# Two load orders and a new set of plan priorities in a convolution-and-attention kernel

## The chip, the core and the metric

The kernel runs on one core of one Trainium2 chip. A core has TensorE (PE; its weight loads are shown apart as PEld), VectorE (DVE), ScalarE (ACT), GpSimd (POOL) and SyncE (SP), each of which takes its own instructions in order. SP, and here and there POOL and ACT, issue DMAs. The metric is the device time of one execution in microseconds (us); less is better. Times of the program are the median of several executions, and one execution is recorded by the hardware profiler.

## What is computed

Two branches work on the same input x (`A_q`, 2048 rows of 640) and are mixed by a gate:

```
g = sigmoid((x * gate_w).sum(-1))
kv = (4-tap causal convolution of A_k along the rows) * A_v
y = irfft(rfft(kv padded to 4096) * rfft(ssm_k padded to 4096))[:2048] + kv * ssm_D
a = x * y
q, k, v = x @ wqkv                     # 32 heads of 20
b = softmax(q . k over 8 keys, 2 rows apart, backwards) @ v, then @ wo
out = g * a + (1 - g) * b
```

Branch a is a long convolution of each of 640 channels; branch b is attention in a narrow dilated window.

## The kernel before

**Stages.** In the order in which they mostly run:

- x is transposed (`trx`), projected to v (`psv`, in two halves of the columns, evicted to `VW`) and to q and k (`pj`, evicted to `Gs` and `sH`). `fragger` (L616) moves pieces of q and k by POOL DMAs into sets of four heads (`qb`, `kb`), eight sets in all, three buffers.
- For each set `score_gen` computes scores (`sc`), ScalarE exponentiates them (L676, `ET`), `pv_gen` multiplies by v (`O`), and VectorE normalises into `oS` (L714, L716).
- VectorE meanwhile makes kv by `conv` in four row blocks, from block 3 down to block 0 (taps and additions of 1.49 us each). Each finished block is stored to DRAM (`st..`), from where kv is loaded again in another layout (`kv<-kv_scr`).
- The filter `ssm_k` is loaded in two halves (`load_h`, each eight DMAs of 160 KB in runs of 128 bytes) over the space of k in `Hb`; POOL adds ssm_D to it (`h_diag`, L802, once for each half).
- `transform` does a two-stage Fourier transform, first of the filter ("h", into `Hs`), then of kv ("u", into `X`): first-stage units (L738) and second-stage units (L760). The second stage multiplies by the matrix G, loaded into `Gs` once the pieces of q and k there are moved. Groups 0 to 2 of five make pass 0, groups 3 and 4 pass 1.
- `swaps` (L826) copies each transformed filter group with its two partition halves exchanged (the turned spectrum). The copy of group 4 is made in two halves, since its place in `X` is group 0's turned copy; its first half is issued after product block 1 of pass 0, its second half after block 3 (events m01, m03).
- `mults` (L848) forms the products in place: L858 (spectrum by spectrum into Hs) and L862 (by the turned copy into X), four blocks for each pass. L858 overwrites what the swap reads.
- `inverse1` (L865) needs the products of its pass: 20 units of 16 matmuls, twelve for pass 0, eight for pass 1. `inverse2` (L930) needs all of inverse1, the table T (`load_t`, after the last product m13) and q, which `load_q` (L903) brings and `qscale` (L923) scales by the gate.
- `otrans` (L885) transposes oS into `Hb` (`tr`), `outproj` (L978) multiplies by wo (`op`), ScalarE scales to `room`, POOL DMAs bring that to `bl`, `adds` adds it to q times y, and the sums are stored.

**What sets the order.** Nothing of it is written out by hand. Each stage is a generator that asks for an engine with a cost and a list of events it depends on (`Req`); `Plan.run` (L208) always grants the request with the smallest start time plus 120 ns times the priority of its generator (`PR`, L146, less is sooner), and only then is the instruction emitted. So each engine's program order comes out of the plan's own clock. A `"S"` request is a DMA on SP's queue, `"G"` a step on POOL. Evictions ask for "AD": ScalarE or VectorE, whichever the plan's clock has ready first; the `..lean` entries shift that choice. An event that a request waits for is a time in the plan. On the chip the waits are those that the data need (a tile written, read, or reused). The plan also hands out the four pairs of PSUM banks.

Of the kernel before, what the change touches and what calls it, by code (L numbers as in the profile page):

```python
# [142 lines left out]
LAT = {("P", "A"): 230.0, ("P", "D"): 230.0, ("A", "P"): 120.0, ("D", "P"): 120.0, ("A", "D"): 100.0, ("D", "A"): 100.0}  # L143


PR = {'warm': -10.0, 'loads': 0.0, 'o_slot': -41.5, 'fragger': -30.7, 'score_gen': -0.4, 'pv_gen': -0.8, 'masks': 1.1, 'wcopy': 3.5, 'halo_gen': -13.7, 'conv': 17.2, 'transposes': 1.3, 'vproj': 2.4, 'gate': 2.4, 'qkproj': 3.1, 'h_diag': 16.3, 'h_stream': 1.9, 'open_p3': 26.5, 'swaps': -47.2, 'u_stream': 7.3, 'mults': -6.7, 'inverse1': 11.0, 'otrans': 10.8, 'outproj': 6.2, 'load_t': 18.2, 'load_q': 8.6, 'qscale': 0.8, 'adds': -3.0, 'inverse2': 25.0, 'vproj1': 4.5, 'vevict': -4.9, 'qevict': -6.0, 'opearly': 14.6, 'oplate': 22.1, 'vlean': 5.0, 'qlean': -169.0, 'slean': 204.0, 'ilean': 93.0, 'olean': 20.0, 'uh': 17.9}  # L146
HEAD = dict(A=130.0, D=60.0)


# [100 lines left out]
def kernel(  # L250
# [91 lines left out]
    def ev(name):  # L342
        if name not in E:
            E[name] = Ev()
        return E[name]
# [10 lines left out]
    def loads():  # L356
        def load(name, dst, src, nb, run, deps=()):
            g = yield Req("S", 300.0 + nb / run * 0.5, deps, move=us(nb, run))
            nc.sync.dma_start(dst, src)
            mark(name, g)  # L360

        def load_x(c, k0=0, k1=4):
            yield from load(f"x{c}{k0}", xS[:, 4 * c + k0:4 * c + k1, :], xq4[:, c // 2, 4 * (c % 2) + k0:4 * (c % 2) + k1, :],
                            163840 * (k1 - k0), 1280)

        def nat(src, a):
            return raw(src, 4 * a * D, [[16 * D, 128], [1, 4 * D]])

        yield from load("ident", ident[:], ca["ident"].ap(), 32768, 256)
        yield from load_x(0, 0, 2)  # L370
        yield from load_x(0, 2, 4)
        yield from load("Wv0", Wv[:, :, 0:320], W3[:, :, 2, 0:320], 409600, 640)
        yield from load_x(1)
        yield from load_x(2)
        yield from load_x(3)
        def load_w(w, part, c0, c1):
            yield from load(f"W{w}{part}", Wqk[:, :, w, c0:c1], W3[:, :, w, c0:c1], 1280 * (c1 - c0), 2 * (c1 - c0))

        def load_k(a):
            yield from load(f"k{a}", Hb[:, 4 * a * D:4 * (a + 1) * D], nat(k2, a), 655360, 5120)  # L380

        def load_v(a):
            yield from load(f"v{a}", kvs[:, 4 * a * D:4 * (a + 1) * D], nat(v2, a), 655360, 5120, [ev("vgo")])

        for part, c0, c1 in (("a", 0, 128), ("b", 128, D)):
            for w in range(2):
                yield from load_w(w, part, c0, c1)
            if part == "a":
                yield from load("wr", pa[:].rearrange("p t c -> p (t c)"), raw(A_shift_k, 0, [[0, 128], [1, 4 * D]]), 655360, 5120)
        yield from load_k(3)  # L390
        yield from load_k(2)
        yield from load_v(3)
        yield from load_k(1)
        yield from load_v(2)
        yield from load_k(0)
        yield from load_v(1)
        yield from load_v(0)
        yield from load("Wv1", Wv[:, :, 320:640], W3[:, :, 2, 320:640], 409600, 640)

        def load_h(half):  # L400
            deps = [ev(f"st{a}{c}") for a in ((2, 3) if half == 0 else (0, 1)) for c in range(2)]
            for q in range(4):
                for c in range(2):
                    yield from load(f"h{half}{q}{c}", st["hv"](half)[32 * q:32 * q + 32, :, c, :],
                                    raw(A_ssm_k, (160 * q + 80 * c + 40 * half) * S, [[64, 32], [S, 40], [1, 64]]), 163840, 128, deps)

        def store_kv(a):
            src = Hb[:, 4 * a * D:4 * (a + 1) * D].rearrange("p (q c x) -> p q c x", q=4, c=2)
            for c in range(2):
                yield from load(f"st{a}{c}", raw(kv_scr[:], (4 * c * S + 4 * a) * 80, [[16 * 80, 128], [S * 80, 4], [1, 320]]),  # L410
                                src[:, :, c, :], 327680, 640, [ev(f"conv{a}")])

        yield from store_kv(3)
        yield from store_kv(2)
        yield from load_h(0)
        yield from store_kv(1)
        yield from store_kv(0)
        for jb in range(4):
            for d, h in zip(pieces(Gs[:, 2048 * jb:2048 * (jb + 1)]), pieces(cf["G"].ap()[:, 2048 * jb:2048 * (jb + 1)])):
                yield from load(f"G{jb}", d, h, 262144, 1024, [ev("stg21"), ev("stg30"), ev("stg31")])  # L420
            ev(f"G{jb}").t += 2000.0
        yield from load_h(1)
        stored = [ev(f"st{a}{c}") for a in range(4) for c in range(2)]
        for c in range(2):
            for m in range(4):
                yield from load(f"kv{c}", kvs[:, 5120 * c + 1280 * m:5120 * c + 1280 * (m + 1)],
                                raw(kv_scr[:], c * 4 * S * 80 + 1280 * m, [[5120, 128], [1, 1280]]), 327680, 2560, stored)
        wo = p0.tile([128, NDT, D], BF, name="wo", tag="wo")
        st["wo"] = wo
        yield from load("wo", wo[:], B_wo.rearrange("(t p) n -> p t n", p=128), 819200, 1280, [ev("vproj1")])  # L430
# [185 lines left out]
    def fragger():  # L616
        todo = {}
        for t in range(NT):
            for w in range(2):
                for h in range(4 * t, 4 * t + 4):  # L620
                    for f in range(DH * h // 128, (DH * h + DH - 1) // 128 + 1):
                        todo.setdefault(t, []).append((f, w, h))
        rest = {}
        for v in todo.values():
            for f, w, h in v:
                rest[(f, w)] = rest.get((f, w), 0) + 1
        for t in range(NT):
            for f, w, h in sorted(todo[t]):
                yield Req("G", 1.0, [ev(f"pj{f}{w}")])
                stg, evs, free = stgs[(f, w)]  # L630
                f0 = 128 * f
                wd = QW if w == 0 else KW
                fa, fb = max(DH * h, f0), min(DH * h + DH, f0 + 128)
                r0 = 32 * (h % 4) + fa - DH * h
                dst = (qsets if w == 0 else ksets)[t % 3]
                deps = list(evs) + ([ev(f"sc{t - 3}")] if t >= 3 else [])
                g = yield Req("G", 510.0, deps, move=us((fb - fa) * wd * 2, 4200) * 1.9)
                nc.gpsimd.dma_start(dst[r0:r0 + fb - fa, 0:wd], stg[fa - f0:fb - f0, 0:wd])  # L638
                if (t, f, w, h) == (0, 0, 1, 3):
                    nc.gpsimd.memset(kvs[0:1, 12 * D:12 * D + 1], 0.0)  # L640
                    mark("vgo", g)
                rest[(f, w)] -= 1
                if not rest[(f, w)]:
                    free.t, free.eng = g.done.t, "X"
                    mark(f"stg{f}{w}", g)
            mark(f"set{t}", g)
        mark("frag", g)


# [176 lines left out]
    def swaps():  # L826

        for g in range(NG):
# [10 lines left out]
            for hf in range(2):  # L839
                yield Req("S", 0.0, deps + [ev(f"m0{2 * hf + 1}")])  # L840
                for p in (0, 64):
                    r = yield Req("S", 700.0, move=us(262144, 512) * 1.9)
                    d, h = (x.rearrange("p (m n) -> p m n", n=512)[:, :, 256 * hf:256 * hf + 256] for x in (turned(g)[p:p + 64], st["HA"][64 - p:128 - p, g, :]))
                    nc.sync.dma_start(d, h)
                for k in range(2):
                    mark(f"hw{g}{2 * hf + k}", r)

    def mults():  # L848
        for ps_, (g0, n, m) in enumerate(PASS):
# [51 lines left out]
        st["bl"] = bl  # L901

    def load_q():  # L903
        yield Req("G", 1.0, [ev("us1")])
        qg = p0.tile([128, 16, D], BF, name="qg", tag="kv")
        st["qg"] = qg
        for a in range(2):
            for g in range(4):
                r = yield Req("S", 900.0, [ev("us1")], move=us(327680, 1280) * 1.4)
                for t in range(2):  # L910
                    nc.sync.dma_start(st["qg"][32 * g:32 * g + 32, 8 * a + t:8 * a + 8:2, :],
                                      raw(x2, (16 * g + 8 * a + t) * D, [[64 * D, 32], [2 * D, 4], [1, D]]))
            mark(f"qg{a}", r)
            ev(f"qg{a}").t += 3000.0
# [167 lines left out]
```

## Time and profile before

| | us |
|---|---|
| median of 5 runs | 241.79 |
| lowest and highest run | 239.98, 243.14 |
| the profiled execution | 241.57 |
| its span, first to last instruction | 239.8 |

Busy time in four stretches of the profiled execution (us of 20):

| from to | PE | DVE | ACT | PE clock | DMA share |
|---|---|---|---|---|---|
| 20 to 40 | 19.5 | 12.2 | 15.4 | 1.00 | 0.77 |
| 80 to 100 | 19.8 | 16.2 | 18.5 | 1.00 | 0.31 |
| 100 to 120 | 15.5 | 15.3 | 18.0 | 0.57 | 0.98 |
| 160 to 180 | 18.0 | 18.7 | 20.0 | 1.00 | 0.82 |
| 200 to 220 | 20.0 | 9.0 | 12.8 | 0.96 | 0.30 |

The clock is the share of full speed that TensorE was granted. An engine that is busy all the time in a stretch sets its length, or one that it waits for does; the busy share alone doesn't say which, and a matmul's end is modelled.

The exponentials (L676) end at 127.4. The first second-stage unit of the filter starts at 130.8, the first of kv at 155.8. The products of pass 0 end at 179.7, those of pass 1 at 198.8; inverse1 ends at 207.8, the last out projection at 225.9.

### The profile page before, as it was taken

The page shows a single profiled execution, that of the slowest core. Times are in us where ns is not written, and L with a number is a line of the kernel's source. Part 1 is how long each engine was busy: PE and PEld are TensorE (multiplying, and loading weights), DVE is VectorE, ACT ScalarE, POOL GpSimd, SP SyncE. Part 2 cuts the span into 40 slices and gives each one's busy share as a digit, 9 for nine tenths or more (in the row PEclk, how much of TensorE's full clock was granted, in tenths as well). Part 3 has the DMA queues.
Part 4 walks back from the last instruction along what each step waited for, and adds up shares of the span by engine and source line. Part 5 has one row for each costly group of instructions (what it writes and reads, how often), then busy time and mean ns, then how long its engine had stood idle before and what let it go on. Part 6 is the DMA issues. An engine that isn't in the chain of part 4 may idle for free. (4 is left out here: it accounts for less than half of the span.)

```text
span 239.8 us, 8121 instructions
## 1 busy us (share of the span) xinstructions
PE 209.4 (87%) x3526; PEld 157.3 (66%) x3526; DVE 172.5 (72%) x214; ACT 183.6 (77%) x225; POOL 67.8 (28%) x137
## 2 busy tenths in 40 slices
PE   7999999999999999887875989989899969999800
PEld 3865645555555566575655778878689959989700
DVE  0667457998797797877774999999998095069760
ACT  4439588779899898889994998999999965943520
POOL 8803711396706053140000000000303020047520
PEclk9999999999999999955555899999999997999955
DMA  6997499677779622499899708996599916015872
GB/s 187 355 329 286 105 303 320 210 186 204 204 141 188 180 53 63 123 188 207 149 152 284 281 3 184 204 202 119 117 218 200 182 30 207 13 57 160 233 217 56
DMA packets 52579, 42.57 MB, mean 178 GB/s; under 512 B 27216, under 2 KB 47824, under 8 KB 52544
## 3 DMA queue, kind: packets, MB, share of 16 engines
q1 hardware_dynamic: 47664, 32.70, 56.6%
q0 software_dynamic: 4688, 9.03, 14.5%
q8 instruction: 27, 0.44, 0.9%
q10 hardware_dynamic: 192, 0.33, 0.5%
q14 instruction: 8, 0.07, 0.1%
HBM read 23.51 MB, written 5.25 MB: 120 GB/s over the span
## 5 line engine op out<-in xcount | busy, mean ns | idle before, releaser
L676 ACT ACTIVATE ET<-sc 128x726 bf16<-128x726 f32 (+1 forms) x80 | 64.9, 862 | 5.8 <-PE sc L668 5.4
L602 PE MATMUL pj<-xT,Wqk 128*128 128x363 bf16 (+3 forms) x250 | 48.4, 343 | 0.0
L1004 POOL DMA_DIRECT2D bl<-room x32 | 16.7, 528 | 81.7 <-ACT room L995 81.7
L602 PEld LDWEIGHTS <-Wqk 128*128 128x128 bf16 x250 | 22.9, 97 | 18.4
L279 DVE CAST Hs<-s 128x1024 bf16<-128x1024 f32 (+1 forms) x26 | 28.6, 1144 | 4.4 <-PE s L738 4.3
L277 ACT CAST X<-s 128x1024 bf16<-128x1024 f32 (+1 forms) x32 | 28.0, 997 | 0.2 <-PE s L738 0.2
L540 PE MATMUL psv<-Wv,xT 128*128 128x320 bf16 x170 | 24.9, 299 | 0.0
L988 PE MATMUL op<-wo,Hb 128*128 128x320 bf16 x160 | 23.9, 301 | 0.6 <-ACT X L277 0.5
L875 PE MATMUL i<-M,Hs 128*128 128x128 bf16 x160 | 21.9, 235 | 2.5 <-DVE Hs L858 2.3
L277 ACT CAST X<-i 128x1024 bf16<-128x1024 f32 x20 | 19.8, 1080 | 4.8 <-PE i L875 4.8
L875 PEld LDWEIGHTS <-Hs 128*128 128x128 bf16 x160 | 20.9, 151 | 2.6 <-DVE Hs L858 2.5
L668 PE MATMUL sc<-qb,kb 31*128 31x121 bf16 x544 | 18.7, 242 | 4.4 <-ACT ET L676 1.2
L875 PE MATMUL i<-M,X 128*128 128x128 bf16 x160 | 21.8, 235 | 0.5 <-DVE X L862 0.5
L988 PEld LDWEIGHTS <-Hb 128*128 128x128 bf16 x160 | 21.3, 145 | 1.3 <-issue 0.4
L760 PEld LDWEIGHTS <-Gs 64*128 64x128 bf16 x512 | 18.4, 95 | 5.3 <-issue 4.6
L875 PEld LDWEIGHTS <-X 128*128 128x128 bf16 x160 | 20.8, 151 | 0.8 <-DVE X L862 0.7
L995 ACT ACTIVATE room<-op,omg 128x640 bf16<-128x640 f32 x16 | 13.2, 825 | 10.3 <-PE op L988 8.6
L638 POOL DMA_DIRECT2D qb<-Gs x21 | 11.5, 551 | 31.7 <-ACT Gs L277 20.3
L668 PEld LDWEIGHTS <-kb 31*128 31x128 bf16 x544 | 10.3, 102 | 15.3 <-issue 12.5
L540 PEld LDWEIGHTS <-xT 128*128 128x128 bf16 x170 | 16.0, 98 | 6.6 <-issue 0.2
L277 ACT CAST Hs<-s 128x1024 bf16<-128x1024 f32 (+1 forms) x18 | 15.4, 912 | 3.7 <-PE s L738 2.3
L702 PEld LDWEIGHTS <-ET 128*128 128x128 bf16 x544 | 16.0, 100 | 3.4 <-issue 1.9
(77 smaller groups left out, 351.4 us busy)
## 6 DMA issues: line engine op xcount, KB each, us to landing
X<-Hs SPq DMA_DIRECT2D x16, 256.0 KB, 6.5
Hb<-in_A_k_dram SPq DMA_DIRECT2D x4, 640.0 KB, 10.4
kv<-in_A_v_dram SPq DMA_DIRECT2D x4, 640.0 KB, 12.3
kv_scr<-Hb SPq DMA_DIRECT2D x8, 320.0 KB, 4.4
Hb<-in_A_ssm_k_dram SPq DMA_DIRECT2D x16, 160.0 KB, 4.5
kv<-kv_scr SPq DMA_DIRECT2D x8, 320.0 KB, 5.0
bl<-room POOLq DMA_DIRECT2D x32, 80.0 KB, 3.4
qg<-in_A_q_dram SPq DMA_DIRECT2D x16, 160.0 KB, 7.2
```

Source lines behind the costliest of these rows:

```text
L277: nc.scalar.copy(dst, src)
L279: nc.vector.tensor_copy(dst, src)
L540: nc.tensor.matmul(ps[:, bb, 0:320], lhsT=xT[:, dt, BP * (b0 + bb):BP * (b0 + bb) + 128], rhs=Wv[:, dt, c0:c0 + 320], start=(dt == 0), sto ...
L602: nc.tensor.matmul(ps[:, i, 0:n], lhsT=Wqk[:, dt, w, 128 * ft:128 * ft + 128], rhs=rhs, start=(dt == 0), stop=(dt == NDT - 1))
L668: nc.tensor.matmul(scs[h4 // 2][:, h4 % 2, BP * bb:BP * bb + BP], lhsT=kb[r:r + DH + NF, 128 * b:128 * b + 128], rhs=qb[r:r + DH + NF, BP ...
L676: nc.scalar.activation(ETs[e][:, :, 0:nw], scs[hf][:, :, 0:nw], ACT.Exp, scale=SCALE)
L702: nc.tensor.matmul(O[:, o0:o0 + 21], lhsT=ET[:, hh, BP * bb:BP * bb + 128], rhs=VW[:, b, 4 * t + h4, :], start=True, stop=True, skip_group ...
L760: nc.tensor.matmul(ps[:, c, 0:64 * n * m].rearrange("p (a j l) -> p a j l", j=m, l=16)[:, :, jj, :], lhsT=G[rows, j, rr, :], rhs=raw(a, 20 ...
L875: nc.tensor.matmul(o, lhsT=piece(A[:, g:g + 1, :])[:, 0, c, :, :, 8 * oc + il].rearrange("p q j -> p (q j)"), rhs=M[:, k, :], start=(k == ...
L988: nc.tensor.matmul(op[:, k, 0:320], lhsT=raw(a, HS * (t % 2) + t // 2, [a.ap[0], [8, 128]]), rhs=wo[:, ft, 320 * k:320 * k + 320], start=( ...
L995: nc.scalar.activation(blt, op[:, :, 0:320], ACT.Copy, scale=omg[:, gcol(t):gcol(t) + 1])
L1004: nc.gpsimd.dma_start(bl[32 * gg:32 * gg + 32, t - 1:t + 1, :].rearrange("p t c -> p (t c)"), raw(row, 0, [[4 * pitch, 32], [1, 1280]]))
```

## The change

Three edits of the plan's input; no operation is added or taken away.

- The filter's later half (`load_h(1)`) stands before the matrix G in the list of loads, and depends, beside its stores, on a new event `fraggo`: the time at which POOL has issued the last piece of q and k. G follows it. A surcharge of 2000 on G's landing is dropped.
- `load_q` depends on a new event `swapped`: the time at which SP has issued the second half of the last turned copy.
- All priorities but two (`warm`, `loads`) are new.

```diff
--- before.py
+++ after.py
@@ -143,7 +143,7 @@
 LAT = {("P", "A"): 230.0, ("P", "D"): 230.0, ("A", "P"): 120.0, ("D", "P"): 120.0, ("A", "D"): 100.0, ("D", "A"): 100.0}
 
 
-PR = {'warm': -10.0, 'loads': 0.0, 'o_slot': -41.5, 'fragger': -30.7, 'score_gen': -0.4, 'pv_gen': -0.8, 'masks': 1.1, 'wcopy': 3.5, 'halo_gen': -13.7, 'conv': 17.2, 'transposes': 1.3, 'vproj': 2.4, 'gate': 2.4, 'qkproj': 3.1, 'h_diag': 16.3, 'h_stream': 1.9, 'open_p3': 26.5, 'swaps': -47.2, 'u_stream': 7.3, 'mults': -6.7, 'inverse1': 11.0, 'otrans': 10.8, 'outproj': 6.2, 'load_t': 18.2, 'load_q': 8.6, 'qscale': 0.8, 'adds': -3.0, 'inverse2': 25.0, 'vproj1': 4.5, 'vevict': -4.9, 'qevict': -6.0, 'opearly': 14.6, 'oplate': 22.1, 'vlean': 5.0, 'qlean': -169.0, 'slean': 204.0, 'ilean': 93.0, 'olean': 20.0, 'uh': 17.9}
+PR = {'warm': -10.0, 'loads': 0.0, 'o_slot': -37.2, 'fragger': -11.1, 'score_gen': -1.0, 'pv_gen': -0.4, 'masks': 6.2, 'wcopy': -16.1, 'halo_gen': 0.5, 'conv': 12.3, 'transposes': -4.4, 'vproj': 1.2, 'gate': -2.3, 'qkproj': 1.3, 'h_diag': 6.6, 'h_stream': 1.5, 'open_p3': 16.0, 'swaps': -46.7, 'u_stream': 6.5, 'mults': 0.7, 'inverse1': 8.7, 'otrans': -14.3, 'outproj': 4.8, 'load_t': 25.8, 'load_q': 12.9, 'qscale': 0.7, 'adds': -9.2, 'inverse2': 13.2, 'vproj1': 3.2, 'vevict': -1.0, 'qevict': -27.5, 'opearly': 13.1, 'oplate': -21.9, 'vlean': 69.0, 'qlean': -76.0, 'slean': 161.0, 'ilean': 215.0, 'olean': -155.0, 'uh': 19.3}
 HEAD = dict(A=130.0, D=60.0)
 
 
@@ -398,7 +398,7 @@
         yield from load("Wv1", Wv[:, :, 320:640], W3[:, :, 2, 320:640], 409600, 640)
 
         def load_h(half):
-            deps = [ev(f"st{a}{c}") for a in ((2, 3) if half == 0 else (0, 1)) for c in range(2)]
+            deps = [ev(f"st{a}{c}") for a in ((2, 3) if half == 0 else (0, 1)) for c in range(2)] + [ev("fraggo")] * half
             for q in range(4):
                 for c in range(2):
                     yield from load(f"h{half}{q}{c}", st["hv"](half)[32 * q:32 * q + 32, :, c, :],
@@ -415,11 +415,10 @@
         yield from load_h(0)
         yield from store_kv(1)
         yield from store_kv(0)
+        yield from load_h(1)
         for jb in range(4):
             for d, h in zip(pieces(Gs[:, 2048 * jb:2048 * (jb + 1)]), pieces(cf["G"].ap()[:, 2048 * jb:2048 * (jb + 1)])):
                 yield from load(f"G{jb}", d, h, 262144, 1024, [ev("stg21"), ev("stg30"), ev("stg31")])
-            ev(f"G{jb}").t += 2000.0
-        yield from load_h(1)
         stored = [ev(f"st{a}{c}") for a in range(4) for c in range(2)]
         for c in range(2):
             for m in range(4):
@@ -644,6 +643,7 @@
                     free.t, free.eng = g.done.t, "X"
                     mark(f"stg{f}{w}", g)
             mark(f"set{t}", g)
+        x = ev("fraggo"); x.t = plan.at["G"]
         mark("frag", g)
 
 
@@ -844,6 +844,7 @@
                     nc.sync.dma_start(d, h)
                 for k in range(2):
                     mark(f"hw{g}{2 * hf + k}", r)
+        x = ev("swapped"); x.t = plan.at["S"]
 
     def mults():
         for ps_, (g0, n, m) in enumerate(PASS):
@@ -901,12 +902,12 @@
         st["bl"] = bl
 
     def load_q():
-        yield Req("G", 1.0, [ev("us1")])
+        yield Req("G", 1.0, [ev("us1"), ev("swapped")])
         qg = p0.tile([128, 16, D], BF, name="qg", tag="kv")
         st["qg"] = qg
         for a in range(2):
             for g in range(4):
-                r = yield Req("S", 900.0, [ev("us1")], move=us(327680, 1280) * 1.4)
+                r = yield Req("S", 900.0, [ev("us1"), ev("swapped")], move=us(327680, 1280) * 1.4)
                 for t in range(2):
                     nc.sync.dma_start(st["qg"][32 * g:32 * g + 32, 8 * a + t:8 * a + 8:2, :],
                                       raw(x2, (16 * g + 8 * a + t) * D, [[64 * D, 32], [2 * D, 4], [1, D]]))
```

Both new events carry a time and nothing else; they make no wait on the chip.

**The order that comes out of it**, from the two built programs. SP's queue (same DMAs, moved):

| before | after |
|---|---|
| k3, k2, v3, k1, v2, k0, v1, v0, Wv half 1, gate out and in | k3, k2, gate out and in, v3, k1, v2, k0, v1, v0, Wv half 1 |
| stores of kv 1 and 0, G, filter half 1, kv | stores of kv 1 and 0, filter half 1, G, kv |
| turned half 0 of group 4, q x12, turned half 1, q x4, T | turned half 0, turned half 1, q x16, T |

TensorE: the same matmuls. In front the first projections of q and k come after 30 instead of 40 of the v projection, the gate's 20 between them. From the first filter unit to the second stage the two orders are alike. The six units of `otrans`, spread over the transform of kv before (15 matmuls here and there), stand in one block inside the transform of the filter, before its last 7 second-stage units of pass 0. In the end:

```
before  ... op10 s2.u32 i1x16 s2.u16 op10 i1x176 op10 i1x128 op20 i2x96 op20 i2x96 ...
after   ... op10 s2.u48 op10 s2.u32 i1x320 op30 i2x96 op20 i2x96 ...
```

(numbers are matmuls; s2.u second stage of kv, i1 and i2 the two inverse stages). Before, six of the 16 out projections stand ahead of inverse1's end, after, five.

VectorE and ScalarE:

| | before | after |
|---|---|---|
| evictions of the v projection on VectorE | 2 (one of 320) | 7 (two of 320) |
| query mask copies on VectorE | 0 | 1 |
| evictions of `tr` on VectorE / ScalarE | 3 / 3 | 5 / 1 |
| casts of inverse1 on VectorE / ScalarE | 0 / 20 | 6 / 14 |
| `qscale` | 8 between the products of block 2 of pass 1, 8 after the last | 16 after the last product |
| casts of inverse1 among the products of pass 1 | 0 | 1 |

POOL: the filter's first diagonal (L802) stands before the pieces of set 5, before it stood after those of set 6.

## The prediction

> **What bounds the kernel now.** I read the chain of waits first, then the waits, then SP's queue, VectorE's timeline and the windows around the two places that the change names. The chain's last third runs through the q loads:
>
> ```profile
> 170.79 0.91 PE s L760 x16
> 171.69 0.26 SPq L911
> ...
> 171.99 5.42 DMA qg<-in_A_q_dram
> ...
> 177.43 7.42 DMA qg<-in_A_q_dram
> ...
> 184.87 7.97 DMA qg<-in_A_q_dram
> ...
> 193.24 2.45 DVE qg L927 x8
> ...
> 198.28 9.54 PE i L875 x127
> 207.82 2.72 PE op L988 x20
> ```
>
> Columns: start, length, what. TensorE restarts at 198.28 with the last eight units of inverse1, which need the products of pass 1; the q lines before it are not a need for q, but q in the way of something. SP's queue tells why q comes into it (start, length, issues):
>
> ```profile
> 99.79 5.34 SPq L359 DMA_DIRECT2D Gs<-cf_G  x8
> 105.17 18.18 SPq L359 DMA_DIRECT2D Hb<-in_A_ssm_k_dram  x8
> ...
> 169.08 2.18 SPq L844 DMA_DIRECT2D X<-Hs  x2
> 171.36 7.89 SPq L911 DMA_DIRECT2D qg<-in_A_q_dram  x12
> 179.87 2.16 SPq L844 DMA_DIRECT2D X<-Hs  x2
> 182.07 3.11 SPq L911 DMA_DIRECT2D qg<-in_A_q_dram  x4
> ```
>
> The second half of the last turned spectrum is issued as soon as its product is ready (179.87), but behind twelve q loads. Who waits for it, and for the filter's later half, in the waits (total, times, longest):
>
> ```profile
> POOL Hb L802 <- DMA Hb<-in_A_ssm_k_dram: 23.0, 1, 23.0
> ...
> DVE Hs L858 <- DMA X<-Hs: 6.4, 1, 6.4
> ...
> PE s L738 <- POOL Hb L802: 2.5, 1, 2.5
> ```
>
> VectorE's timeline has the price, windows of TensorE the consequence:
>
> ```profile
> 191.30 1.23 DVE L858 TENSOR_TENSOR Hs<-X,Hs 128x2048 bf16<-128x2048 bf16 x1 [6.42 <-DMA X<-Hs]
> 192.63 0.69 DVE L862 TENSOR_TENSOR X<-X,sH 128x1024 bf16<-128x1024 bf16 x1
> 193.24 2.45 DVE L927 TENSOR_SCALAR qg<-qg,g_nat 128x640 bf16<-128x640 bf16 x8
> ```
>
> ```profile
> 195.00:198.00 3.00, 0.50 (x3) 0.14 (x1) 2.90 (x6) 0.80 (x1) 1.65 (x4) 1.00 0.10 39
> 198.00:201.00 3.00, 2.72 (x26) 2.72 (x27) 3.00 (x10) 0.86 (x1) 0.43 (x1) 0.54 0.43 140
> ```
>
> Columns: PE, PEld, DVE, ACT, POOL busy, clock, DMA share, GB/s. TensorE idles 3.15 us (195.1 to 198.28) and then runs at 0.54 of its clock: the last 8 units take 9.54 us where 8 x 16 matmuls at 62.7 ns (their spacing at 183 us) take 8.0. Elsewhere: to 98 us TensorE is full (19.5 to 19.8 of every 20 us from 20 to 100); from 98 to 127.4 ScalarE's exponentials set the pace; from 131 to 180 ScalarE and VectorE evict side by side without pause; from 199 TensorE again.
>
> **What the Trainium skill says.** "DMA: Bandwidth & Descriptors", Queues, rings and completion order: each ring's descriptors are consumed in order, and SP's DMAs share one row of rings. The trace agrees: the pair issued on an empty queue at 169.08 holds the quickest landing of the four (4.2 us), the pair behind q is in only at 191.3, 11.4 us after its issue. Same page, Anatomy of one DMA: waits happen on the issuing sequencer; so SP's order matters, and in the built program the filter's later half gets no wait on a fragment at all, only on the stores. "TensorE: Matmul & The Clock Gate", Part 1: an idle window of about 3.4 us halves the clock until some 3.4 us of work have passed. The trace agrees in kind: 0.54 after 3.15 us idle, a little less than the page's window.
>
> **The change part by part.** All times against the profiled execution, span 239.8, 1.77 us outside it (241.57); the median shown is 0.22 above that.
>
> *A. The front, re-ordered (to 98 us).* VectorE takes 5 more evictions of the v projection (7 for 2) and one query mask; ScalarE loses those and gains a transpose and a projection eviction. TensorE's work is unchanged, so only waits count. Its second group of transposes now comes after 10 instead of 20 projections, at 8.4; the xS loads' median landing of 6.4 us after the issue at 2.75 gives 9.15: wait 0.75. Before the first scores it has about 0.5 us less other work, and they hang on the fragments: 0.5. Taken: +1.2; bounds -0.5 (ScalarE is 3 to 4 us lighter) and +3. The gate's round trip now stands before the v loads on SP: 4 + 5 small DMAs (1.8 + 2.4 us), the first behind k, drained at 24.4 (VectorE's first tap); v's first load goes at about 29.3 for 28.27, k's two others and the rest of v behind it. Needed at 41.8: hidden. On POOL the filter's first diagonal moves ahead of set 5's fragments (72.9 before): these wait for the filter's landing, about 79; their scores run at 102: hidden, 15 us to spare.
>
> *B. Filter's later half ahead of the matrix G.* Eight loads took 8.1 us to issue (first half) and land in 4.5; even if the last convolution still ends at 98.6, they start at 104 after its stores and are in at 117, where 127.8 was. G follows: issued by 117, median landing 4.8, first piece about 119. The 2.54 us wait at 125.9 goes; what is late next is the exponentials, to 127.4, so the second stage starts at 128.6 for 130.83: -2.2. Bounds -2.5 and 0 (G in only at the 127.8 that both took together). The h loads now lie across set 7's fragments (100.9 to 104.8), whose scores come at about 118: hidden. After A the second stage starts at 129.8, -1.0.
>
> *C. Eviction stage to the last product of pass 0.* Counted in the two orders: VectorE one Hs cast less (-1.1), two transposed-o evictions more (+2.2), two first-stage casts for two second-stage ones (+0.5): +1.6. ScalarE: +1 Hs (0.95), -2 transposes (3.36), -2 +2 casts (-0.3), +1 out projection (0.69): -2.0. All six transposes now stand inside the filter's transform, so its turned copies start about 3 us later (146.4 for 143.3); the third group lands at about 165.6 (162.5 + 3.1), first used at 167.4: just hidden. VectorE ends pass 0 at 179.74 - 1.0 + 1.6 = 180.3; ScalarE its spectrum casts at 182.7 - 1.0 - 2.0 = 179.7. So inverse1 runs from 179.8 without the pieces between its first two units (182.63 before).
>
> *D. q behind the last turned half.* Issued at 180.4, second DMA 1.1 later, landing 4.2 to 6.8: 186.4. VectorE then needs 1.23+0.69+0.68+1.21+0.69+0.68 and one inverse1 eviction (1.1) that the plan puts there; the 2.45 us of q scaling is gone from between. Products done at 192.7 for 198.8. The cost: q's 16 loads (2.62 MB) start at 182.6 for 171.4. At the 200 GB/s of the slices from 171 to 189 they are in at 195.9, T (1.05 MB, behind them on SP and in the rings) at 201.1. Its reader inverse2 comes at 205.1 (below): 4 us to spare.
>
> *E. The end.* inverse1: 12 units of 1.0 from 179.8 to 191.9, next 8 from 192.8 to 200.8, no idle window and so no clock dip, for 207.82. From there the old trace takes 18.04 us to the last out projection's end (225.86); one more projection is now behind (1.44): 220.3, **-5.6**. After it everything is as before (13.9 us: last store path). Span 234.2, time 236.0, with the 0.22 to the median 236.2. The new priorities by themselves have no cost but through these orders.
>
> **The rivals.** *1. The same within 1%:* the gain is taken by a later landing, q and T. For: they start 11 us later, and T is last in the rings. Against: at 200 GB/s there are 4 us to spare. From 164 GB/s (3.67 MB in 22.4 us) inverse2 waits; at 140 it starts 3.8 us late: 240.0. The turned copies that C leaves with under 2 us of cover would, 4 us late, give the same number.
>
> *2. Slower:* VectorE's in-order queue in the front. The five added evictions stand between 1.49 us taps and additions; a bank pair held that long (there are four) stops TensorE, which has no slack to 98 us. For: the fullness of both. Against: seven such evictions behind one tap each are 7 x 1.49 = 10.4 us at most, if no bank pair is ever to spare; two of them stood on VectorE before and cost TensorE nothing that its waits show. From 5.6 us in all it is slower than before; at 1.2 us for each of the seven, 8.4: 244.6. A front that starts its filter transform after 106 us decides for it.
>
> *3. It doesn't do what it says:* the fragment event is only a time in the plan; on the chip the order in SP's queue acts alone. If the stores are the last to arrive anyway, only D and E remain, and A: -3.4, 238.4.
>
> **Numbers.** The likeliest, 236.2, has 0.50 (own range 233.5 to 238.3); rival 3, 0.13; rival 1, 0.15; rival 2, 0.22. About 1% (2.4 us) is what a measurement here can tell from no change: the runs spread from 239.98 to 243.14. Faster by more: 0.50 + 0.13 = 0.63; within: 0.15; slower: 0.22. The range, 233 to 245, leaves out the worst half of rival 2 and a front that gains.
>
> **What would show it.** Right: X<-Hs at L845's pair landing in 4 to 7 us and no wait of several us on it by L859; the clock at 1.0 to the end of inverse1; POOL's diagonal long before TensorE asks; inverse1 in one run ending near 201. Wrong: first-stage filter matmuls starting later than 100 us (A); a wait of inverse2 on T, or of the scaling on q, beyond 205 (rival 1); L863 waiting on X<-Hs near 167 (C); TensorE waiting on VectorE's VW evictions before 98 (rival 2).

## The result, and the profile after

| | before | changed kernel |
|---|---|---|
| median (runs) | 241.28 us (46) | 243.33 us (25) |
| ratio of times, 95% interval | | 1.0126 [1.0104, 1.0149] |

The change makes the kernel **slower by about 1%, 2 to 3 us**, where 5.6 us less was forecast. The medians are of all runs and lie 2.05 us apart; the ratio, here and in the experiments, leaves out runs more than 1.5% above the fastest of the same kernel, 24 of before's 46 among them. The first profiled execution of the changed kernel took 246.72 us, 1.4% above its median; so the lines below are from a second profiled execution of the same kernel, of 244.21 us (span 242.4; run e12 below). Before's span was 239.8.

First the chain of waits (start, length, what), the part that ran through the q loads before:

```profile
163.16 4.47 ACT X L277 x7
...
170.15 1.75 DVE Hs L859
171.92 1.29 DVE X L863 x2
173.22 0.88 DVE X L279
174.14 0.66 PE s L738 x8
...
188.86 20.24 PE i L876 x320
209.10 4.08 PE op L989 x30
```

The q loads are gone from it and inverse1 is one run of 20.24 us, as meant. But it starts at 188.86, where 179.8 was forecast. Ahead of it stands the first product (L859; 858 before), at 170.15. It started at 162.90 before.

SP's queue shows both load edits at work, and the delay (start, length, issues):

```profile
102.08 11.28 SPq L359 DMA_DIRECT2D Hb<-in_A_ssm_k_dram  x8
113.61 5.35 SPq L359 DMA_DIRECT2D Gs<-cf_G  x8
...
149.95 13.47 SPq L835 DMA_DIRECT2D X<-Hs  x12
...
179.37 8.61 SPq L844 DMA_DIRECT2D X<-Hs  x4
188.08 12.94 SPq L912 DMA_DIRECT2D qg<-in_A_q_dram  x16
```

The filter's later half is under way at 102 and q comes behind all the copies. The twelve turned copies of pass 0 (L835), though, start at 149.95. Before:

```profile
143.29 13.11 SPq L835 DMA_DIRECT2D X<-Hs  x12
```

VectorE's timeline of e12 has what hangs on them (in brackets the idle time before the instruction, and what the profile says ended it):

```profile
161.24 4.08 DVE L279 CAST X<-s 128x768 bf16<-128x768 f32 x4 [0.97 <-PE s L760]
170.13 1.76 DVE L859 TENSOR_TENSOR Hs<-X,Hs 128x3072 bf16<-128x3072 bf16 x1 [4.81 <-ACT X L277]
...
193.13 1.22 DVE L859 TENSOR_TENSOR Hs<-X,Hs 128x2048 bf16<-128x2048 bf16 x1 [0.18 <-DMA X<-Hs]
```

The third line is the wait of 6.42 us that the q edit was to remove: 0.18 is left. The second is a new one of 4.81 us, at the head of the products. In before the same place has 0.43, also put down to ScalarE:

```profile
162.90 1.76 DVE L858 TENSOR_TENSOR Hs<-X,Hs 128x3072 bf16<-128x3072 bf16 x1 [0.43 <-ACT X L277]
```

TensorE's timeline of e12 tells why the copies are late, and what the new wait does to it:

```profile
137.60 4.71 PE L895 MATMUL tr<-ident,oS 121*128 121x121 bf16 x85
142.27 0.51 PE L760 MATMUL s<-Hs,Gs 64*128 64x192 bf16 x8
144.09 0.51 PE L760 MATMUL s<-Hs,Gs 64*128 64x192 bf16 x8 [1.32 <-ACT Hb L277]
145.24 0.51 PE L760 MATMUL s<-Hs,Gs 64*128 64x192 bf16 x8 [0.64 <-DVE Hb L279]
146.14 6.88 PE L760 MATMUL s<-Hs,Gs 64*128 64x192 bf16 x160 [0.40 <-DVE Hb L279]
...
174.14 0.66 PE L738 MATMUL s<-F1b,kv 64*128 64x128 bf16 x8 [5.23 <-DVE X L279]
```

The 85 output transposes stand in one block before the last units of pass 0 of the filter. After 4.71 us of their own they cost 2.36 us of waits, since the units behind them need the PSUM that the transposes' evictions (1.1 us on VectorE, 1.67 on ScalarE each) hold. From 137.60 to 146.14 are 8.54 us for three second-stage units; the trace before has, at the same place,

```profile
138.63 0.51 PE L760 MATMUL s<-Hs,Gs 64*128 64x192 bf16 x8
139.54 6.61 PE L760 MATMUL s<-Hs,Gs 64*128 64x192 bf16 x176 [0.40 <-DVE Hs L279]
```

three units in 1.6 us (the fourth starts at 140.20). The difference, 7.0 us, is most of the delay of the copies: from the first second-stage unit of the filter to the first copy are 20.3 us in e12 and 12.5 in before. The rest, 0.8 us, lies in the four units that follow, which take 2.5 us for 1.7; the granted clock was at half from 145.7 to 149.1 in e12, and at 1.0 there in before. The last line of TensorE's timeline is the second half of the damage: VectorE, blocked before its first product, evicts nothing, and TensorE stands for 5.23 us.

### The profile page after: what moved, and what is told of

The parts are those of the page before. It is cut to its first block, busy times and chain, and to the rows that moved or that the text cites. A ratio compares the mean times of both kernels' runs of the same rounds, so it can differ in the third digit from the quotient of the medians.

```text
span 244.9 us, 8131 instructions
## 1 busy us (share of the span) xinstructions
PE 210.3 (86%) x3526; PEld 158.7 (65%) x3526; DVE 182.7 (75%) x221; ACT 176.2 (72%) x218; POOL 67.4 (28%) x137
## 3 DMA queue, kind: packets, MB, share of 16 engines
HBM read 23.51 MB, written 5.25 MB: 117 GB/s over the span
## 4 chain that ended last, share of the span: by engine, by line
PE 51%; ACT 12%; DMA 12%; DVE 11%; SPq 6%; issue 5%; POOL 1%; DVEq 0%; ACTq 0%
PE pj L601 13%; PE i L876 8%; PE psv L539 7%; PE op L989 7%; ACT ET L676 5%; SPq L835 5%; PE O L702 3%; PE s L760 3%; ACT X L277 3%; PE sc L668 3%; DMA Wv<-in_B_wqkv_dram 2%; DMA kv<-kv_scr 2%; DMA Gs<-cf_G 2%; PE tr L895 2%; DVE pa L494 2%
## 5 line engine op out<-in xcount | busy, mean ns | idle before, releaser
L676 ACT ACTIVATE ET<-sc 128x726 bf16<-128x726 f32 (+1 forms) x80 | 64.1, 863 | 4.4 <-PE sc L668 4.3
L279 DVE CAST Hs<-s 128x1024 bf16<-128x1024 f32 (+1 forms) x25 | 27.8, 1143 | 2.3 <-PE s L738 1.1
L539 PE MATMUL psv<-Wv,xT 128*128 128x320 bf16 x170 | 26.8, 307 | 2.6 <-DMA Wv<-in_B_wqkv_dram 1.6
L989 PE MATMUL op<-wo,Hb 128*128 128x320 bf16 x160 | 24.7, 309 | 0.4 <-DVE X L279 0.3
L760 PEld LDWEIGHTS <-Gs 64*128 64x128 bf16 x512 | 21.1, 102 | 6.0 <-issue 5.3
L277 ACT CAST Gs<-pj 128x968 bf16<-128x968 f32 (+5 forms) x18 | 13.5, 748 | 10.0 <-PE pj L601 9.8
L876 PE MATMUL i<-M,Hs 128*128 128x128 bf16 x160 | 20.2, 227 | 0.2 <-ACT X L277 0.2
L876 PEld LDWEIGHTS <-Hs 128*128 128x128 bf16 x160 | 20.1, 149 | 0.1
L876 PEld LDWEIGHTS <-X 128*128 128x128 bf16 x160 | 20.1, 149 | 0.1
L876 PE MATMUL i<-M,X 128*128 128x128 bf16 x160 | 20.2, 226 | 0.0
L637 POOL DMA_DIRECT2D qb<-Gs x21 | 10.5, 507 | 31.1 <-ACT Gs L277 22.1
L277 ACT CAST Hs<-s 128x1024 bf16<-128x1024 f32 (+1 forms) x19 | 16.4, 920 | 3.1 <-PE s L760 3.0
```

Of the source, the lines that this page charges most:

```text
L277: nc.scalar.copy(dst, src)
L279: nc.vector.tensor_copy(dst, src)
L539: nc.tensor.matmul(ps[:, bb, 0:320], lhsT=xT[:, dt, BP * (b0 + bb):BP * (b0 + bb) + 128], rhs=Wv[:, dt, c0:c0 + 320], start=(dt == 0), sto ...
L676: nc.scalar.activation(ETs[e][:, :, 0:nw], scs[hf][:, :, 0:nw], ACT.Exp, scale=SCALE)
L760: nc.tensor.matmul(ps[:, c, 0:64 * n * m].rearrange("p (a j l) -> p a j l", j=m, l=16)[:, :, jj, :], lhsT=G[rows, j, rr, :], rhs=raw(a, 20 ...
L876: nc.tensor.matmul(o, lhsT=piece(A[:, g:g + 1, :])[:, 0, c, :, :, 8 * oc + il].rearrange("p q j -> p (q j)"), rhs=M[:, k, :], start=(k == ...
```

## The experiments

All runs were timed against before on the same chip. "Both load edits" are the hunks of `load_h`, G and `load_q` shown above, with their two events; the medians are of all runs.

| run | load edits | priorities | median us | ratio, 95% interval |
|---|---|---|---|---|
| e1 | filter | old | 239.37 | 0.9979 [0.9947, 1.001] |
| e2 | q | old | 238.55 | 0.9885 [0.9842, 0.9929] |
| e3 | both | old | 236.0 | 0.9801 [0.9758, 0.9845] |
| e4 | none | new | 248.13 | 1.0312 [1.0267, 1.0358] |
| e5 | both | front new, late old | 237.41 | 0.9845 [0.9793, 0.9897] |
| e6 | both | front old, late new | 243.86 | 1.0112 [1.0057, 1.0166] |
| e7 | both | new, block after pass 0 | 237.45 | 0.9851 [0.9796, 0.9905] |
| e8 | both | new, first product by group | 239.77 | 0.998 [0.9956, 1.0005] |
| e9 | both | old, `otrans` new | 240.11 | 0.9979 [0.9954, 1.0004] |
| e10 | both | new, `otrans` old | 249.94 | 1.0357 [1.0297, 1.0417] |
| e11 | both | old, `otrans` new, block after pass 0 | 236.0 | 0.9767 [0.9722, 0.9812] |
| e12 | both | new (the changed kernel) | 243.17 | 1.0111 [1.0083, 1.0139] |

And from each profiled execution, in us: the end of the last exponential (L676), from there to the first turned copy's issue, from that to the start of the first product, the end of inverse1 and the span:

| run | exponentials end | to the first copy | copy to product | inverse1 ends | span |
|---|---|---|---|---|---|
| before | 127.4 | 15.9 | 19.6 | 207.8 | 239.8 |
| e1 | 127.4 | 13.6 | 19.6 | 205.2 | 237.2 |
| e2 | 128.4 | 13.4 | 19.6 | 200.4 | 234.8 |
| e3 | 129.5 | 13.4 | 19.4 | 201.5 | 236.0 |
| e4 | 129.4 | 20.7 | 19.6 | 223.0 | 246.7 |
| e5 | 128.5 | 13.3 | 20.0 | 200.6 | 235.0 |
| e6 | 134.7 | 16.2 | 20.2 | 209.8 | 243.2 |
| e7 | 129.1 | 13.6 | 22.6 | 203.7 | 235.6 |
| e8 | 128.4 | 20.4 | 15.3 (third part 19.4) | 204.3 | 237.7 |
| e9 | 126.9 | 20.8 | 20.1 | 207.0 | 238.2 |
| e10 | 129.4 | 13.5 | 19.6 | 203.2 | 247.6 |
| e11 | 126.5 | 13.3 | 22.6 | 202.0 | 232.6 |
| e12 | 128.7 | 21.2 | 20.2 | 209.1 | 242.4 |

### Load edits or priorities (e1 to e4)

e1, e2 and e3 have before's line of priorities; e1 and e2 one load edit each (the lines that set the events are left out here):

```diff
 e1
+        yield from load_h(1)
         for jb in range(4):
...
-            ev(f"G{jb}").t += 2000.0
-        yield from load_h(1)
 e2
-        yield Req("G", 1.0, [ev("us1")])
+        yield Req("G", 1.0, [ev("us1"), ev("swapped")])
...
-                r = yield Req("S", 900.0, [ev("us1")], move=us(327680, 1280) * 1.4)
+                r = yield Req("S", 900.0, [ev("us1"), ev("swapped")], move=us(327680, 1280) * 1.4)
```

e4 has the new line of priorities and nothing else.

> The old priorities with one load edit: the filter's later half ahead of the fourth operand G, q where it was. The order of TensorE's work is that of before. Theory (load edits are gains, the priorities lose): the 2.5 us wait of TensorE on GpSimd's later diagonal goes and little comes in its place, so 2.0 to 2.7 us less than before, about 238.9 at 241.3 for before (ratio 0.989 to 0.992). Rival (the load edits themselves cost, because G or kv now comes late): 0 to +3 us, and second-stage filter matmuls or scores that wait on a DMA of G or kv.

> The old priorities with the other load edit: q and the matrix T behind the swaps of the last turned group, the filter's halves where they were. Theory: VectorE's wait of 6.4 us on the turned copies of the second pass goes, inverse1 runs without its gaps, and the whole takes 4.5 to 6 us less than before, about 236 (ratio 0.975 to 0.981). Rival (q and T now late): inverse2 waits on T or q beyond the end of inverse1 for 3 us or more, and the gain is 2 us or less (ratio above 0.99).

> Both load edits under the old priorities: the change without its new priorities. Theory: the two gains add, 7 to 8.5 us less than before, about 233.5 (ratio 0.965 to 0.972); the first turned swaps start near 141 us and the first product of filter and spectrum near 160. Rival (the load edits cost, alone or together): 241 to 245 as the changed kernel has it (ratio 1.00 to 1.015).

> The new priorities with the loads where they were. Theory (the priorities lose what the load edits win, and more): the front is 3 to 5 us later, the block of output transposes inside the filter's transform holds the turned copies back by about 5 us, the wait on the later diagonal and that on the second pass's copies stay: 248 to 252 (ratio 1.028 to 1.045). Rival (the load edits are the loss): 241 or less (ratio 1.00 or less).

The signs came out as the theory had them: both edits together gain 2.0%, the new priorities by themselves lose 3.1%. In microseconds of the medians the two edits bring 4.8 under the old priorities (240.82 to 236.0, runs e3 and before) and 4.8 under the new (248.13 to 243.33, e4 and the changed kernel): no interaction shows.

The sizes were too large in three of four. **e1 brings little**: 0.2%, with an interval from 0.5% less to no gain (1.45 us between the medians, for 2.0 to 2.7 expected). A possible reason lies in e2, which has the loads of the filter in before's order. GpSimd's second diagonal in e2 (start, length; bracket as above):

```profile
125.93 0.57 POOL L802 TENSOR_TENSOR Hb<-Hb,Dz 128x80 bf16<-128x80 bf16 x1 [20.54 <-DMA Hb<-in_A_ssm_k_dram]
```

In before it stood at 127.80. The same eight loads landed 1.9 us sooner in this execution, and TensorE, which waited 2.54 us in before, shows no wait there; only its weight load has one of 0.2. e4, with the same load order, shows no such wait either. So the wait that the prediction took from before's profile is there in some executions and not in others. How often is not shown: the profiled execution of e2 was the fastest of its six (236.63, median 238.55), and e3, which adds the filter edit to e2, is 2.0 us better than e2 by the ratios, 2.6 by the medians. So the edit is worth 0.5 to 2.6 us, and these runs don't settle it further. e2 gains 1.2% where 1.9% or more was expected; its inverse1 ends 7.4 us sooner (200.4 for 207.8), but 34.4 us of tail follow for 32.0; one out projection more, left behind it, is 1.5 us of that.

### Front or late priorities (e5, e6)

Both load edits; of the priorities e5 takes the seventeen of the front from the new line, e6 the twenty others (pieces of the one line):

```diff
 e5
-'o_slot': -41.5, 'fragger': -30.7, 'score_gen': -0.4,
+'o_slot': -37.2, 'fragger': -11.1, 'score_gen': -1.0,
...
-'vevict': -4.9, 'qevict': -6.0, 'vlean': 5.0, 'qlean': -169.0,
+'vevict': -1.0, 'qevict': -27.5, 'vlean': 69.0, 'qlean': -76.0,
 e6
-'h_diag': 16.3, 'h_stream': 1.9, 'open_p3': 26.5,
+'h_diag': 6.6, 'h_stream': 1.5, 'open_p3': 16.0,
...
-'otrans': 10.8, 'outproj': 6.2,
+'otrans': -14.3, 'outproj': 4.8,
...
```

> Both load edits, the new priorities for the work of the front alone (projections, fragments, scores, masks, transposes, evictions), the old ones for the filter's transform, the swaps, the inverse and the output products. Theory (the front and the output transposes each cost, the second more): 2.5 to 4.5 us above the run with both load edits under the old order (236.0), so 238.5 to 240.5 (ratio 0.990 to 1.00); the turned swaps start about 4 us later than there. Rival (the front is the whole loss): 242.5 to 244 (ratio 1.007 to 1.015).

> Both load edits, the old priorities for the front, the new ones for all that is late. Theory: the block of output transposes lies inside the filter's transform again, the turned swaps start 4 to 6 us later than in the run with both edits under the old order, the first product waits for the third group's copy: 239 to 241.5 (ratio 0.990 to 1.003). Rival (the front is the whole loss): 235 to 237 (ratio 0.975 to 0.985).

The front costs 1.4 us against e3 (237.41 for 236.0), less than the 2.5 to 4.5 expected, and their intervals overlap; the copies start no later than in e3 (141.9 for 142.9), where 4 us later was expected. The late priorities lose 7.9 (243.86), more than expected. e6 isn't the late half alone: the new weights also put filter units earlier among the scores, so its exponentials end at 134.7. The copies still start at 150.9, and the first product waits 4.99 us.

### The block of transposes (e7, e9, e10, e11)

e7 moves the block behind pass 0 of the filter, with all else as in the changed kernel:

```diff
-        yield Req("G", 1.0, [ev("oS"), ev("hs1")])
+        yield Req("G", 1.0, [ev("oS"), ev("hs1"), ev("h0o31")])
...
-            g = yield Req("P", 5 * nb * 53.0, [ev("oS")], take=1, ins=5 * nb)
+            g = yield Req("P", 5 * nb * 53.0, [ev("oS"), ev("h0o31")], take=1, ins=5 * nb)
```

e9 is e3 with `'otrans': -14.3` for 10.8, e10 the changed kernel with 10.8 for -14.3, e11 is e9 with e7's edit.

> The changed kernel with one thing moved: the block of output transposes waits until the first pass of the filter's transform is done, so it lies between that pass and the second. Theory (the block delays the turned copies): the swaps start about 5 us sooner than 152.4, the first product about 5 us sooner than 172.5, and the whole takes 3.5 to 5 us less than the changed kernel: 238 to 240 (ratio 0.988 to 0.995). Rival (the block's time is only moved, since TensorE is the bound there): 242.5 to 244 (ratio 1.006 to 1.013).

> Both load edits under the old priorities, but for one number: the priority of the output transposes is the new one. TensorE's order up to the last exponential stays that of the old order; the 85 transposes lie in one block inside the filter's transform instead of behind it. Theory (this block is the loss): the swaps start 7 us later than in the run with both load edits under the old order, the first product waits 3 to 5 us for the third group's copy, and the whole takes 5 to 7 us more than that run's 236.0: 241 to 243 (ratio 1.00 to 1.008). Rival (the loss needs the other late priorities too, the products' and evictions' among them): 236 to 238.5 (ratio 0.98 to 0.99).

> The changed kernel but for one number: the priority of the output transposes is the old one, so they are spread over the end of the second stage and the start of the inverse, some between two stretches of the inverse. Theory (the block is the loss): the swaps start about 7 us sooner after the last exponential than in the changed kernel, no wait before the first product; the inverse has gaps of some 2 us for the transposes and more output products are left behind it, so 237 to 240 (ratio 0.98 to 0.995). Rival (the other new priorities lose as much): 242 to 244 (ratio 1.005 to 1.015).

> Both load edits, the old priorities but for the output transposes, whose one block waits until the first pass of the filter's transform is done. Theory (what costs is only that the block lies ahead of the first pass's end): swaps as early as with the old order, no wait before the first product, 235 to 237.5 (ratio 0.975 to 0.985). Rival (a block of 85 transposes costs wherever it lies, by its evictions): 238 to 242 (ratio 0.988 to 1.005).

**e7** takes 5.9 us off the changed kernel (237.45 for 243.33), a little more than the theory's 5. The step to the first copy falls from 21.2 to 13.6. **e9** puts it back from the other side: that single number takes e3's 13.4 to 20.8 and costs 4.1 us, below the 5 to 7 expected but well outside the rival's range. **e11** has the block as one piece and costs nothing against e3: 236.0 both. VectorE waits 1.86 us among its evictions there as in the changed kernel, but now behind the last spectrum of pass 0, where the copies, 19.2 us from the first issue to the last landing, run beside it. So it isn't the transposes, nor their being in one block, but what stands behind them: with the block ahead of the last seven units, the first copy comes 20.4 to 21.2 us after the exponentials in e4, e8, e9 and e12; without it, 13.3 to 15.9 in before and in the runs that have it elsewhere. (In e6 the exponentials themselves end late.)

**e10 missed for both theories.** The copies did start early (13.5) and inverse1 ended 5.9 us sooner than in e12, but the span grew by 5.2. The first product still waited, 5.25 us, where no wait was expected, and here the profile puts it down to the copies (`DMA X<-Hs`). TensorE's timeline and VectorE's waits after 200:

```profile
203.05 0.70 PE L895 MATMUL tr<-ident,oS 121*128 121x121 bf16 x10
203.58 0.45 PE L989 MATMUL op<-wo,Hb 128*128 128x320 bf16 x2
```

```profile
DVE qg L1013 <- DMA bl<-room: 15.5, 6, 5.8
```

The last transposes now come only behind the whole of inverse1, so none of the 16 out projections stands ahead of its end (five do in the changed kernel), and the last additions wait 15.5 us in all for their rows. Five projections more behind inverse1 are some 7.5 us (1.5 each) of the 11 by which the tail grows (44.4 for 33.3). The early block has this use: it lets the out projections start early. It was put a few units too soon.

### What the first product waits for (e8), and a second profile (e12)

```diff
+                one = ps_ == 0 and k == 0
+                if not one:
-                nc.vector.tensor_tensor(blocks(st["HA"]), blocks(st["UA"]), blocks(st["HA"]), ALU.mult)
+                    nc.vector.tensor_tensor(blocks(st["HA"]), blocks(st["UA"]), blocks(st["HA"]), ALU.mult)
                 for g in range(g0, g0 + n):
+                    if one:
+                        H_ = block(st["HA"][:, g, :])
+                        nc.vector.tensor_tensor(H_, block(st["UA"][:, g, :]), H_, ALU.mult)
```

> The changed kernel with its first product in place over three groups split into one product for each group, so that the first overwrites only the group whose turned copy was made first. Theory (VectorE's 4.9 us before that product is the wait until the third group's copy has read the filter's spectrum): the first of the three starts at 168 to 170 instead of 172.5, the stretch of products loses part of its head, and the whole takes 1 to 3 us less than the changed kernel: 240.5 to 242.3 (ratio 0.997 to 1.005). Rival (the wait is on ScalarE's eviction, as the page names it): the wait of 4.9 us stays before the first of the three, 243.5 or a little more (ratio 1.01 to 1.016).

> The changed kernel as it is, for a second profile of it. Theory (some 2 us of the late front in its first profile belong to that execution): from the first projection of V to the first exponential 26.8 to 27.9 us, as in the four runs that share its front, not 28.95; the swaps about 20.5 us after the last exponential; the ratio again 1.010 to 1.015. Rival (the front as a whole costs 4 us or more with these loads): 28.5 us or more again.

VectorE in e8:

```profile
164.09 0.69 DVE L865 TENSOR_TENSOR Hs<-X,Hs 128x1024 bf16<-128x1024 bf16 x1
...
168.28 0.69 DVE L865 TENSOR_TENSOR Hs<-X,Hs 128x1024 bf16<-128x1024 bf16 x1 [1.44 <-DMA X<-Hs]
```

The first part starts without a wait, straight behind the last eviction, though the order of ScalarE's evictions is the same; the third waits 1.44 us and is now put down to the copy. That settles which releaser the 4.81 us had: the copy of group 2, not ScalarE. The gain is 3.6 us, more than the 1 to 3 expected, since TensorE's wait falls too (2.30 us for 5.23).

The trace of e3 shows how tight it was all along; its chain of waits:

```profile
154.51 7.35 DMA X<-Hs
162.24 1.77 DVE Hs L859
```

The last copy of pass 0 lands at 161.86, the product starts at 162.24. In e12 the landing is at 169.76 and the product at 170.13, in before at 162.53 and 162.90; in the eleven profiles other than those of e7, e8 and e11 the product starts 0.37 or 0.38 us behind the last landing. "Copy to product" in the table above is 19.4 to 20.2 in every run but three: e7 and e11, where VectorE has the transposes to evict first, and e8, whose third part has it. The twelve issues and the last landing set it, so the first product moves with the first copy, nearly us for us.

e12 gives the second profile: from the first v projection (7.17) to the first exponential (34.25) are 27.1 us, inside the 26.8 to 27.9 expected; the copies are 21.2 us behind the exponentials for the 20.5 expected.

## Why the prediction was wrong

**A, the front: right in size, as far as the runs can tell.** Forecast +1.2; the last exponential ends 1.3 later in e12 than before. One pair says little: with the old front it ends between 126.5 and 129.5 (before, e1, e2, e3, e9, e11), with the new one between 128.4 and 129.4 (e4, e5, e7, e8, e10, e12), the means 1.2 apart. e5 against e3 gives 1.4 us of time. The mark that it set itself, first filter units not after 100 us, was missed (100.98) without the front being what lost; e3, faster and with the old front, has 101.66. TensorE shows no wait on VectorE's evictions of `VW`, so rival 2's mechanism didn't occur; its direction came from elsewhere.

**B, the filter's later half: right in the trace, its size as a gain open.** The second stage starts at 129.69, 1.1 before the old trace's, for a forecast 1.0 after A. For the 2.2 us of gain the runs give 0.5 (e1 alone) to 2.6 (e3 against e2), since the wait that was to go is in before's profile and not in e2's and e4's.

**C: the step that failed.** The prediction put the copies at 146.4; they start at 149.95. The second stage began when forecast (129.69 for 129.8); up to the first copy the forecast has 4.1 us more than before (16.6 for 12.5), and 7.8 came. It names neither TensorE's waits for evictions (2.4 us) nor a fall of the clock (0.8). Worse is its sentence "the third group lands at about 165.6 (162.5 + 3.1), first used at 167.4: just hidden". The 167.4 stands for the first reading of that copy, by L862 (165.90 in before, so some 166.5 with the forecast's own shifts of -1.0 and 1.6). But L858, the product before it, overwrites in one instruction the spectra of all three groups that the copies read from, so it too waits for the third copy, and it started at 162.90 before: 0.37 us after the landing. There was no cover. The wait is for the completion: the Trainium skill, "DMA: Bandwidth & Descriptors", Two DMAs through the same engine are not ordered, names the completion semaphore as the ordering a kernel's author has, and its full increment means that the data has landed; e3's landing at 161.86 before the product at 162.24 agrees. So 6.7 us of late copies became 7.2 of late product. e8, whose first product overwrites one group alone, wins 3.6 us back. The products of pass 0 end at 187.80 for the 180.3 forecast. These 7.5 us are most of the 8.2 between the forecast span (234.2) and e12's (242.4). Half of this was within reach: the front section says that L858 overwrites what the swap reads.

**D: right.** From the last product of pass 0 to the last of pass 1 are 11.6 us (187.80 to 199.38), 12.4 forecast, 19.1 before. The half clock of 198.3 to 201.7 in before is gone in e12, as in e2, e3, e5, e7 and e11. T is issued at 201.60 and has landed at 209.99, and inverse2 runs from 213.11 without a wait on T or q, so that half of rival 1 is out. Its other clause, copies with under 2 us of cover landing late, came true by more than it allowed for.

**E: right.** inverse1 takes 20.24 us in one run at full clock (21.0 forecast), one more out projection stands behind it, and 33.3 us follow, for 33.4 forecast.

In sum, the loads gain 4.8 us (e3 against before), and the order loses some 7.3 (243.33 against e3's 236.0): the block 4.1 to 5.9 (e9, e7), the front about 1.4 (e5). What is left, 0 to 1.8 us, was not taken apart further; e12 has 2.2 us more tail than e9, with ten out projections behind the end of inverse1 there and eleven in e12, which fits but was not tried alone. Both kernels are beaten by e3 and e11, at 0.9801 and 0.9767 of before, alike within their intervals.

## What to carry to other kernels

When a transfer is delayed, look for every instruction that needs its completion, those that overwrite its source as well as those that read its result; the first of them sets the cover, and an in-place instruction over several tiles waits for the last tile's transfer. Where a filler is put into a pipeline, ask which transfer the units behind it start: the same 85 transposes cost 4 us or more seven units before the end of a pass and nothing just after it. And a wait of 2 us in one profile may not be there in the next execution of the same loads; only a second profile shows whether its removal is a gain.

## What the runs showed of the hardware

After its wait of 5.23 us TensorE came back at half clock and stayed there longer than after before's wait. Windows of 1 us in e12 (busy PE, PEld, DVE, ACT, POOL, granted clock, DMA share, GB/s):

```profile
173.00:174.00 1.00, 0.00 (x0) 0.00 (x0) 1.00 (x2) 0.00 (x0) 0.00 (x0) 0.51 0.60 103
...
179.00:180.00 1.00, 1.00 (x6) 0.66 (x5) 1.00 (x3) 0.09 (x1) 0.00 (x0) 0.58 0.00 0
180.00:181.00 1.00, 1.00 (x20) 0.78 (x19) 1.00 (x2) 0.55 (x1) 0.00 (x0) 1.00 0.32 66
```

A mean of 0.51 puts the fall to half at 173.0, one of 0.58 the return at 179.84: 6.8 us, though work began again at 174.14. Before has:

```profile
198.00:199.00 1.00, 0.72 (x7) 0.72 (x8) 1.00 (x3) 0.00 (x0) 0.43 (x1) 0.63 0.35 133
...
201.00:202.00 1.00, 1.00 (x14) 1.00 (x13) 0.20 (x1) 0.31 (x2) 0.00 (x0) 0.67 0.97 337
```

The same reading gives 198.26 and 201.66: 3.4 us, half of that. The Trainium skill, "TensorE: Matmul & The Clock Gate", Part 1, explains it: the clock is set by free-running windows of about 3.4 us, and a whole busy one brings full speed back. The traces agree: before restarted at 198.28, as a window began, and e12 1.1 us into one, which didn't count. e9 restarted 0.1 us into one and had 3.4 us at half clock; e6, e10 and e4 restarted 1.6, 1.8 and 2.3 us into one and had 6.8. So of two idle stretches the one that ends badly can cost up to a window more. It works on short waits too: behind the same block of transposes, with waits of 2.0 to 2.4 us in all, the clock fell to half for 3.4 us in e4, e6, e9 and e12, and not in e8.
